# Seven-product stage with its own sum buffers, another product order, a bank-to-bank copy and weight buffers assigned by hand

## The chip, the cores and the metric

The kernel runs on one core of a Trainium2 chip. Its time is the device time of one execution in microseconds; the median of three runs is given. A profiled execution gives the trace, with times counted from its first instruction (the span). Engines are named as in the trace: PE is TensorE's matmuls and PEld its weight loads, DVE is VectorE, ACT ScalarE, POOL GpSimd, SP SyncE.

## The reference

Causal attention over 2 x 12 heads, 448 positions and a head dimension of 64, then two feed-forward layers over the 896 tokens:

```python
x = attention(q, k, v)                       # (896, 768)
r = np.maximum(x @ moe_w_in, 0.0)            # (896, 2048)
x = (s * (r * r) + b) @ moe_w_out            # (896, 768)
gate = 1.0 / (1.0 + np.exp(-(x @ w_gate)))   # (896, 1536)
out = (gate * (x @ w_val)) @ w_out           # (896, 768)
```

All inputs and the output are fp32. The weight matrices are handed over as the two 32-bit words of 64-bit numbers, which the kernel turns into floats itself.

## The kernel before

Tokens lie in the free dimension, in two halves of 448 (`B` = 2, `S` = 448); a matmul multiplies a 128x128 block of weights with a 128x448 block of activations. To keep fp32 accuracy every operand is split into a high and a low part, and a block product is three matmuls: high by high, high by low, low by high.

The stages follow each other on TensorE: attention, `w_in`, `w_out`, then the **seven-product stage** for `w_gate` and `w_val`, then two output stages for `w_out`. The seven-product stage computes, for each of 12 quads `q` (128 columns of the gate and of the value, both token halves), the four 128x448 results by Strassen and Winograd's scheme with seven products instead of eight. Each product has a depth of 3 blocks, so 3 x 3 = 9 matmuls, or 63 a quad. The left factors are combinations of weights: `a`, `b` (halves of the gate), `s1`, `s2` (the sum tile `s12`), `s3`, `s4` (`s34`) and `d` (half of the negated value); the right factors are combinations of activations (`b11`, `t1`, ..., `b22`), kept in `x2_b` and `z_b`. `PARTS` says which pair makes which product. Products 1, 6, 7, 4 are accumulated in bank A, 5 and 3 in bank C, 2 in bank E; after each of 1, 6 and 7 `evacuate` reads the running sum of bank A.

Per quad the weights come about so. SyncE loads `raw` (768 KB, two buffers). `float_steps` makes a float tile `wt` of it: one instruction on ScalarE (L77), four on VectorE (L79 to L91). VectorE adds the tiles to `s12` and `s34` (L593). `halves` splits a tile: ScalarE copies the high part (L102); the low part is either a subtraction on VectorE (L108) or, with `adder`, a negating copy on ScalarE (L105) and a GpSimd transfer that adds the tile to it (L106). `a`, `s12` and `d` take the adder, `s34` the subtraction. `wt`, `s12` and `s34` share a pool of five buffers, the split weights have another pool of five; a pool hands out its buffers in turn, and the first writer waits until the last reader of the old content is done.

The order of products is written out (`seq`), and `LEAD` says how many products ahead each step of a quad's weights stands in the program; within that, a scheduler at build time sets each engine's order. At run time each engine works through its list in order, so that one waiting instruction holds all behind it.

After the stage `split_y` splits the results `y_f` into blocks that are no longer needed (`free`), and two output stages multiply them (L711, L136).

## Time and profile before

| | us |
|---|---|
| median of 3 runs | 575.52 |
| lowest and highest | 573.78, 575.71 |
| profiled execution, own time | 580.73 |
| its span | 579.0 |
| mean granted TensorE clock in it | 0.991 |

The profiled execution lies 1.73 us above its span and 5.21 us above the median. TensorE is busy for 97% of the span, PEld 85%, VectorE 73%, ScalarE 56%. Busy times count an instruction from start to end; matmuls overlap, so that one takes 0.36 us from start to end but the next starts about 0.2 us after it.

### The profile page before, as it was taken

How to read it: one execution, taken by the hardware profiler on the slowest of the kernel's cores; microseconds unless marked ns; L12 is line 12 of the kernel's file. 1: busy time of each engine (PE TensorE's matmuls, PEld its weight loads, DVE VectorE, ACT ScalarE, POOL GpSimd, SP SyncE). 2: the span in 40 equal slices, each digit the busy share in tenths (PEclk: the TensorE clock that was granted, in tenths of full speed). 3: DMA queues.
4: the chain of work that ended last, by engine and by line, in shares of the span. 5: the costliest groups of instructions: out<-in, count | busy, mean ns of one | idle time of the engine just before them, and what ended most of it. 6: DMA issues, size and time to landing. Idle time of an engine off the chain costs nothing.

```text
span 579.0 us, 8350 instructions
## 1 busy us (share of the span) xinstructions
PE 560.4 (97%) x3068; PEld 490.4 (85%) x3069; DVE 421.6 (73%) x798; ACT 326.4 (56%) x622; POOL 73.3 (13%) x129
## 2 busy tenths in 40 slices
PE   8999999999999999999999999999989899999997
PEld 4666789899999999999999988888878789999996
DVE  5899676999999976865527788876777779987100
ACT  7989846776776633332227677665656588235100
POOL 3676600000000000000001111111201110000000
PEclk9999999999999999999999999998989899999999
DMA  7854012344444453233152577775766643456100
GB/s 242 304 167 174 19 60 106 115 158 164 155 144 148 147 170 121 72 137 109 53 112 48 143 182 182 183 178 153 180 171 169 166 94 121 154 167 200 41 33 32
DMA packets 21354, 79.19 MB, mean 137 GB/s; under 512 B 2624, under 2 KB 6080, under 8 KB 21312
## 3 DMA queue, kind: packets, MB, share of 16 engines
q1 hardware_dynamic: 15696, 65.94, 33.8%
q0 software_dynamic: 5184, 11.80, 11.5%
q10 hardware_dynamic: 432, 0.92, 0.5%
q8 instruction: 24, 0.39, 0.3%
q14 instruction: 18, 0.15, 0.1%
HBM read 64.10 MB, written 2.75 MB: 115 GB/s over the span
## 4 chain that ended last, share of the span: by engine, by line
PE 61%; issue 15%; DVE 9%; DMA 7%; ACT 6%; POOL 1%; POOLq 0%; DVEq 0%; ACTq 0%
PE acc L136 40%; PE acc L711 8%; DMA d_lo<-wt 5%; PE po L321 4%; PE tp L299 3%; PE sc L250 3%; DVE wt L91 2%; DVE wt L87 2%; ACT pt L240 2%; ACT wt L77 2%; PE bankA L627 2%; DMA a_lo<-wt 1%; POOL a_lo L106 1%; PE bankC L627 1%; DVE wt L79 1%
## 5 line engine op out<-in xcount | busy, mean ns | idle before, releaser
L136 PE MATMUL acc<-x_b,whi 128*128 128x448 f32 x456 | 130.8, 368 | 0.0
L77 ACT ACTIVATE wt<-raw 128x768 f32<-128x768 f32 (+1 forms) x70 | 62.2, 888 | 65.4 <-DMA raw<-in_w_out 14.3
L136 PE MATMUL acc<-gb,whi 128*128 128x448 f32 x336 | 96.6, 368 | 0.0
L136 PEld LDWEIGHTS acc<-x_b,whi 128*128 128x128 f32 x456 | 85.4, 188 | 8.1 <-ACT whi L102 0.3
L136 PE MATMUL acc<-x_b,wlo 128*128 128x448 f32 x228 | 83.8, 367 | 0.1
L79 DVE TENSOR_SCALAR wt<-wt 128x768 f32<-128x768 f32 (+1 forms) x70 | 38.8, 554 | 47.0 <-ACT wt L77 46.4
L136 PEld LDWEIGHTS acc<-gb,whi 128*128 128x128 f32 x336 | 63.1, 188 | 6.5
L102 ACT ACTIVATE whi<-wt 128x768 fp32r<-128x768 f32 (+1 forms) x46 | 37.5, 815 | 54.5 <-PE acc L136 39.7
L87 DVE SCALAR_TENSOR_TENSOR wt<-raw,wt 128x768 uint32<-128x768 uint32 (+1 forms) x70 | 65.7, 938 | 1.0
L91 DVE SCALAR_TENSOR_TENSOR wt<-raw,wt 128x768 uint32<-128x768 uint32 (+1 forms) x70 | 65.6, 937 | 0.7
L136 PE MATMUL acc<-gb,wlo 128*128 128x448 f32 x168 | 61.8, 368 | 0.0
L108 DVE TENSOR_TENSOR wlo<-wt,whi 128x768 fp32r<-128x768 f32 (+1 forms) x46 | 42.8, 930 | 16.9 <-ACT whi L102 16.8
L106 POOL DMA_DIRECT2D a_lo<-wt x12 | 10.4, 865 | 334.2 <-ACT a_lo L105 229.6
L136 PEld LDWEIGHTS acc<-x_b,wlo 128*128 128x128 f32 x228 | 42.8, 188 | 4.5 <-DVE wlo L108 0.5
L240 ACT ACTIVATE pt<-pt,m 128x320 f32<-128x320 f32 (+6 forms) x84 | 41.7, 500 | 5.5 <-DVE m L237 5.4
L279 POOL TENSOR_SCALAR pt<-pt,r 128x128 f32<-128x128 f32 (+6 forms) x82 | 39.9, 507 | 27.6 <-DVE r L274 21.7
L82 DVE TENSOR_SCALAR wt<-wt 128x768 uint32<-128x768 uint32 (+1 forms) x70 | 38.5, 550 | 1.4
L136 PEld LDWEIGHTS acc<-gb,wlo 128*128 128x128 f32 x168 | 31.5, 188 | 3.1
L237 DVE CUSTOM_DVE_ANT_0 pt<-sc,mask 128x320 f32<-128x320 f32 (+6 forms) x84 | 30.2, 412 | 4.4 <-PE sc L250 4.4
L627 PE MATMUL bankA<-x_b,s_hi 128*128 128x448 f32 x96 | 29.7, 373 | 0.0
L250 PE MATMUL sc<-qk 64*64 64x64 f32 (+6 forms) x336 | 26.0, 410 | 0.8 <-DMA qk<-in_qk 0.7
L102 ACT ACTIVATE s_hi<-s 128x768 fp32r<-128x768 f32 x24 | 20.3, 846 | 11.2 <-PE bankE L627 9.2
(125 smaller groups left out, 1059.8 us busy)
## 6 DMA issues: line engine op xcount, KB each, us to landing
raw<-in_w_in SPq DMA_DIRECT2D x16, 768.0 KB, 4.3
raw<-in_w_gate SPq DMA_DIRECT2D x12, 768.0 KB, 4.3
raw<-in_w_val SPq DMA_DIRECT2D x12, 768.0 KB, 4.9
raw<-in_w_out SPq DMA_DIRECT2D x12, 640.0 KB, 4.1
qk<-in_qk SPq DMA_DIRECT2D x9, 608.0 KB, 5.8
raw<-in_w_out SPq DMA_DIRECT2D x6, 768.0 KB, 4.4
a_lo<-wt POOLq DMA_DIRECT2D x12, 384.0 KB, 3.9
s_lo<-s POOLq DMA_DIRECT2D x12, 384.0 KB, 4.1
```

The source lines that it names most:

```text
L77: nc.scalar.activation(out=f32(tt), in_=f32(high), func=AF.Abs, scale=RAISE)
L79: nc.vector.tensor_scalar(out=f32(tt), in0=f32(tt), scalar1=F64_TINY, scalar2=F64_HUGE, op0=ALU.max, op1=ALU.min,)
L87: nc.vector.scalar_tensor_tensor(out=tt, in0=low, scalar=29, in1=tt, op0=ALU.logical_shift_right, op1=ALU.bitwise_or,)
L91: nc.vector.scalar_tensor_tensor(out=tt, in0=high, scalar=SIGN, in1=tt, op0=ALU.bitwise_and, op1=ALU.bitwise_xor,)
L102: nc.scalar.activation(out=hif, in_=f32(tt), func=AF.Copy)
L108: nc.vector.tensor_tensor(out=lof, in0=f32(tt), in1=f32(hif), op=ALU.subtract)
L136: nc.tensor.matmul(acc[:, :S], w[:, k - k0], m, start=k == 0 and i == 0, stop=k == K - 1 and i == 2)
L240: nc.scalar.activation(out=pc, in_=pc, func=AF.Exp, scale=-1.0, bias=m, accum_out=l)
L250: nc.tensor.matmul(sc[j * D:(j + 1) * D, :n], t["qk"][rows, q0:q0 + D], t["qk"][rows, k0:k0 + n], start=True, stop=True,)
L279: engine.tensor_scalar(out=probs(i, c), in0=probs(i, c), scalar1=st[i]["r"][:, c:c + 1], scalar2=1.0, op0=ALU.mult, op1=ALU.mult,)
L627: nc.tensor.matmul(acc[:, :S], a[:, j], m, start=fresh and j == 0 and n == 0, stop=j == KH - 1 and n == 2, skip_group_check=True,)
L711: nc.tensor.matmul(acc[d, h][:, :S], w[:, k * GROUP + d], m, start=u == 0 and k == 0 and n == 0, stop=u == NF2 // 2 - 1 and k == 1 and n == 2,
```

## The change

- The sums `s12` and `s34` get five places of their own (`s_f`) in a block of activations that is free by then, in place of the pool that they shared with `wt`. The activation blocks are cut in two for this (`ga0`, `ga1`, `gb00`, `gb01`, `gb10`, `gb11`).
- The order of products in a quad becomes 1, 5, 4 (of the quad before), 6, 3 (of the quad before), 2, 7; it was 6, 3 (before), 1 (next), 7, 2, 5 (next), 4. `LEAD` changes with it.
- After product 1 ScalarE copies bank A to bank E, and product 2 is added there by TensorE; the sigmoid then reads bank E. Before, product 1 was copied to SBUF and VectorE added bank E.
- Split weights: `a`/`b` alternate between two buffers, `s12` has one, `s34` alternates between two, `d` has one of its own in `ga1`. `s12` and `d` now use the subtraction, `s34` the adder. `raw` and `wt` keep two and five buffers.
- The blocks for the split outputs are taken from other places.

```diff
--- before.py
+++ after.py
@@ -32,6 +32,7 @@
     B, NP, _, W = qk.shape
     S = outT.shape[1] // B
     AHEAD = 2
+    SLOTS = 5
     READY = 3
     U = 6
     NT = B * S
@@ -44,7 +45,7 @@
 
     const = ctx.enter_context(tc.tile_pool(name="const", bufs=1))
     big = ctx.enter_context(tc.tile_pool(name="big", bufs=1))
-    wp = ctx.enter_context(tc.tile_pool(name="wp", bufs=AHEAD + READY))
+    wp = ctx.enter_context(tc.tile_pool(name="wp", bufs=1))
     ev = ctx.enter_context(tc.tile_pool(name="ev", bufs=4))
     BANKS = {"w": 7, "po": 1}
     dram = ctx.enter_context(tc.tile_pool(name="dram", bufs=1, space=bass.MemoryType.DRAM))
@@ -61,8 +62,14 @@
     def bank(name, tag):
         return ps.tile([P, 512], F32, tag=tag, name=name, bufs=BANKS[tag])
 
+    turns = {}
+
+    def turn(what, n):
+        turns[what] = turns.get(what, -1) + 1
+        return f"{what}{turns[what] % n}"
+
     def load_words(src, n):
-        raw = wp.tile([P, U * P, 2], U32, tag="raw", name="raw", bufs=2)
+        raw = wp.tile([P, U * P, 2], U32, tag=turn("raw", 2), name="raw")
         nc.sync.dma_start(out=raw[:, :n * P], in_=src)
         return raw
 
@@ -71,7 +78,7 @@
 
         nn = n * P
         low, high = raw[:, :nn, 0], raw[:, :nn, 1]
-        t = wp.tile([P, U * P], U32, tag="wt", name="wt")
+        t = wp.tile([P, U * P], U32, tag=turn("wt", SLOTS), name="wt")
         tt = t[:, :nn]
         out.append(t)
         nc.scalar.activation(out=f32(tt), in_=f32(high), func=AF.Abs, scale=RAISE)
@@ -92,10 +99,12 @@
             out=tt, in0=high, scalar=SIGN, in1=tt, op0=ALU.bitwise_and, op1=ALU.bitwise_xor,
         )
 
-    def halves(tt, out, adder=False, name="w"):
-
-        hi = wp.tile([P, U, P], F32R, tag="whi", name=f"{name}hi")
-        lo = wp.tile([P, U, P], F32R, tag="wlo", name=f"{name}lo")
+    def halves(tt, out, adder=False, name="w", slot=None):
+
+        if slot is None:
+            slot = turn("w", SLOTS)
+        hi = wp.tile([P, U, P], F32R, tag=f"{slot}h", name=f"{name}hi")
+        lo = wp.tile([P, U, P], F32R, tag=f"{slot}l", name=f"{name}lo")
         out += [hi, lo]
         nn = tt.shape[1]
         hif, lof = (x.rearrange("p k m -> p (k m)")[:, :nn] for x in (hi, lo))
@@ -151,8 +160,9 @@
 
     x_b = blocks(big, KC * B, "x", "x_b")
     ga = ctx.enter_context(tc.tile_pool(name="ga", bufs=1))
-    ga_b = blocks(ga, AHEAD * B, "ga", "ga_b")
+    ga_b = [blocks(ga, AHEAD * B - 1, "ga0", "ga0"), blocks(ga, 1, "ga1", "ga1")]
     gb_b = []
+    FIRST = (9, NF2)
 
     def pair_of(t, i):
         return t[:, i, 0], t[:, i, 1]
@@ -161,7 +171,12 @@
         return pair_of(x_b, B * k + h)
 
     def at_g(k, h):
-        return pair_of(ga_b, B * k + h) if k < AHEAD else pair_of(gb_b[h], k - AHEAD)
+        if k < AHEAD:
+            n = B * k + h
+            return pair_of(ga_b[0], n) if n < AHEAD * B - 1 else pair_of(ga_b[1], 0)
+        one, two = gb_b[h]
+        k -= AHEAD
+        return pair_of(one, k) if k < FIRST[h] else pair_of(two, k - FIRST[h])
 
 
     def first_evac(f, h, acc):
@@ -476,7 +491,10 @@
                 pass
 
     gb = ctx.enter_context(tc.tile_pool(name="gb", bufs=1))
-    gb_b += [blocks(gb, NF1 - AHEAD, f"gb{h}", f"gb{h}") for h in range(B)]
+    gb_b += [
+        [blocks(gb, n, f"gb{h}{i}", f"gb{h}{i}") for i, n in enumerate((FIRST[h], NF1 - AHEAD - FIRST[h]))]
+        for h in range(B)
+    ]
 
     for f in range(AHEAD, NF1):
         ready = [(*split[f], 0, KC)] if f < AHEAD + READY else units(w_in[f], KC)
@@ -551,7 +569,9 @@
     done[end] = [bank("acc", "w") for _ in range(B)]
     for unit in last_units:
         mm3(done[end][0], unit, NF1, at_g, 0)
-    z_b = blocks(gb, NF1 - AHEAD, "gb0", "z_b")
+    z_b = blocks(gb, FIRST[0], "gb00", "z_b")
+    SUMS = 5
+    s_f = gb.tile([P, SUMS, U * P], F32, tag="gb01", name="s_f")
     for i, key in enumerate(late):
         place[key] = (z_b, i)
     for ty, j in late:
@@ -569,34 +589,37 @@
 
         t = quads[q] = {}
         fl = []
-        yield from drained(float_steps(load_words(w_gate[q], KC), KC, fl))
-        yield from drained(float_steps(load_words(w_val[q], KC), KC, fl, negate=True))
-        tg, tv = fl
         H = KH * P
         one, two = slice(0, H), slice(H, 2 * H)
 
-        def split(tt, names, adder):
+        def split(tt, names, adder, slot):
             out = []
-            for _ in halves(tt, out, adder, names[0] + "_"):
+            for _ in halves(tt, out, adder, names[0] + "_", f"w{slot}"):
                 pass
             for n, ty in enumerate(names):
                 t[ty] = [x[:, n * KH:(n + 1) * KH] for x in out]
 
-        split(tg, ("a", "b"), True)
+        yield from drained(float_steps(load_words(w_gate[q], KC), KC, fl))
+        split(fl[0], ("a", "b"), True, q % 2)
         yield
-        s12 = wp.tile([P, U * P], U32, tag="wt", name="s12")
-        s34 = wp.tile([P, U * P], U32, tag="wt", name="s34")
+        yield from drained(float_steps(load_words(w_val[q], KC), KC, fl, negate=True))
+        tg, tv = fl
+        s12, s34 = (s_f[:, (2 * q + n) % SUMS] for n in range(2))
         for out, x, y in (
-            (s12[:, one], tv[:, one], tv[:, two]), (s12[:, two], s12[:, one], tg[:, one]),
-            (s34[:, one], tg[:, one], tv[:, one]), (s34[:, two], s12[:, two], tg[:, two]),
+            (s12[:, one], f32(tv[:, one]), f32(tv[:, two])), (s12[:, two], s12[:, one], f32(tg[:, one])),
+            (s34[:, one], f32(tg[:, one]), f32(tv[:, one])), (s34[:, two], s12[:, two], f32(tg[:, two])),
         ):
-            nc.vector.tensor_tensor(out=f32(out), in0=f32(x), in1=f32(y), op=ALU.add)
+            nc.vector.tensor_tensor(out=out, in0=x, in1=y, op=ALU.add)
         yield
-        split(s12, ("s1", "s2"), True)
+        split(s12, ("s1", "s2"), False, 2)
         yield
-        split(s34, ("s3", "s4"), False)
+        split(s34, ("s3", "s4"), True, 4 - q % 2)
         yield
-        split(tv[:, two], ("d",), True)
+        d_w = ga.tile([P, 2, KH, P], F32R, tag="ga1", name="d_w")
+        hi, lo = (d_w[:, n].rearrange("p k m -> p (k m)") for n in range(2))
+        nc.scalar.activation(out=hi, in_=f32(tv[:, two]), func=AF.Copy)
+        nc.vector.tensor_tensor(out=lo, in0=f32(tv[:, two]), in1=f32(hi), op=ALU.subtract)
+        t["d"] = d_w[:, 0], d_w[:, 1]
         yield
 
     def drained(steps):
@@ -617,7 +640,7 @@
         wh, wl = quads[q][w]
         xs = x2_at(x)
         key = {1: "A", 6: "A", 7: "A", 4: "A", 5: "C", 3: "C", 2: "E"}[i], q
-        fresh = i in (1, 5, 2)
+        fresh = i in (1, 5)
         if fresh:
             banks[key] = bank(f"bank{key[0]}", "w")
         acc = banks[key]
@@ -632,28 +655,33 @@
     def evacuate(i, q):
 
         A, C, E = (banks[x, q][:, :S] if (x, q) in banks else None for x in "ACE")
-        if i in (1, 6, 7):
+        if i == 1:
+            E = banks["E", q] = bank("bankE", "w")
+            nc.scalar.activation(out=E[:, :S], in_=A, func=AF.Copy)
+        elif i == 2:
+            s = ring[i, q] = r_f[:, ring["n"] % RING]
+            ring["n"] += 1
+            nc.scalar.activation(out=s, in_=E, func=AF.Sigmoid)
+        elif i in (6, 7):
             s = ring[i, q] = r_f[:, ring["n"] % RING]
             ring["n"] += 1
             nc.scalar.activation(out=s, in_=A, func=AF.Copy)
         if i == 7:
             s = ring[7, q]
             nc.vector.tensor_tensor(out=s, in0=C, in1=s, op=ALU.add)
-        elif i in (2, 3):
-            s = ring[1 if i == 2 else 6, q]
-            nc.vector.tensor_tensor(out=s, in0=E if i == 2 else C, in1=s, op=ALU.add)
+        elif i == 3:
+            s = ring[6, q]
+            nc.vector.tensor_tensor(out=s, in0=C, in1=s, op=ALU.add)
             nc.scalar.activation(out=s, in_=s, func=AF.Sigmoid)
-            if i == 3:
-                nc.vector.tensor_tensor(out=y_f[:, B * q + 1], in0=s, in1=ring[7, q], op=ALU.mult)
+            nc.vector.tensor_tensor(out=y_f[:, B * q + 1], in0=s, in1=ring[7, q], op=ALU.mult)
         elif i == 4:
-            nc.vector.tensor_tensor(out=y_f[:, B * q], in0=A, in1=ring[1, q], op=ALU.mult)
-
-    seq = [(1, 0), (2, 0), (5, 0)]
-    for q in range(NF2 + 1):
-        for i, n in ((6, q), (3, q - 1), (1, q + 1), (7, q), (2, q), (5, q + 1), (4, q)):
-            if 0 <= n < NF2 and (i, n) not in seq:
-                seq.append((i, n))
-    LEAD = (9, 8, 6, 5, 3, 0, -2)
+            nc.vector.tensor_tensor(out=y_f[:, B * q], in0=A, in1=ring[2, q], op=ALU.mult)
+
+    seq = [(1, 0), (5, 0), (6, 0), (2, 0), (7, 0)]
+    for q in range(1, NF2 + 1):
+        seq += [(1, q), (5, q), (4, q - 1), (6, q), (3, q - 1), (2, q), (7, q)]
+    seq = [(i, q) for i, q in seq if q < NF2]
+    LEAD = (10, 8, 8, 6, 3, 2, -3)
     todo = sorted(
         (seq.index((1, q)) - lead, q, n) for q in range(NF2) for n, lead in enumerate(LEAD)
     )
@@ -667,18 +695,21 @@
     for unit in last_units:
         mm3(done[end][1], unit, NF1, at_g, 1)
     second_half(d, done[end], ("t2", "t4"))
-    RING = 2 * B * AHEAD
+    RING = 2 * (B * AHEAD - 1)
     ring["n"] = 0
-    r_f = ga.tile([P, RING, S], F32, tag="ga", name="r_f")
-    y_f = gb.tile([P, B * NF2, S], F32, tag="gb1", name="y_f")
+    r_f = ga.tile([P, RING, S], F32, tag="ga0", name="r_f")
+    y_f = gb.tile([P, B * NF2, S], F32, tag="gb10", name="y_f")
+    v_b = blocks(gb, NF1 - AHEAD - FIRST[1], "gb11", "v_b")
     for n, (i, q) in enumerate(seq):
         prepare(n)
         multiply(i, q)
         evacuate(i, q)
 
 
-    free = [(z_b, i) for i in range(len(late), NF1 - AHEAD)]
+    free = [(v_b, i) for i in range(NF1 - AHEAD - FIRST[1])]
     free += [place[ty, j] for ty in ("b11", "t1", "t2", "t3", "b21", "t4", "b22") for j in range(KH)]
+    c_b = blocks(ga, AHEAD * B - 1, "ga0", "c_b")
+    free += [(c_b, i) for i in range(AHEAD * B - 1)]
 
     def at_y(k, h):
         return pair_of(*free[B * k + h])
```


Lines shift: L77 is now L84, L79 to L91 are L86 to L98, L102 to L108 are L111 to L117, L593 is L612, L627 is L650, L711 is L742.

TensorE, where product 1 of a quad begins, before. `bankA_3400` belongs to the new quad, `bankA_3283` to the one before it; `a` is product 1's weight, `s3` product 7's:

```order
L627 MATMUL bankC_3216<-z_b_2963,s3_lo_3175 128x448
L627 MATMUL bankA_3400<-x2_b_2162,a_hi_3294 128x448 x2
L627 MATMUL bankA_3283<-x2_b_2162,s3_hi_3279 128x448 x2
L627 MATMUL bankA_3283<-x2_b_2162,s3_lo_3280 128x448
L627 MATMUL bankA_3283<-x2_b_2162,s3_hi_3279 128x448
L627 MATMUL bankA_3400<-x2_b_2162,a_lo_3295 128x448
L627 MATMUL bankA_3400<-x2_b_2162,a_hi_3294 128x448 x2
L627 MATMUL bankA_3400<-x2_b_2162,a_lo_3295 128x448
L627 MATMUL bankA_3400<-z_b_2963,a_hi_3294 128x448 x2
```

Here the first two matmuls of product 1 need only `a_hi`; three of product 7 follow, then the first that needs `a_lo`. After the change the same place reads so, with `bankA_3416` for the new quad and `bankA_3304` for the one before it, and `d_w` for product 4's weight:

```order
L650 MATMUL bankA_3416<-z_b_2966,a_hi_3280 128x448 x2
L650 MATMUL bankA_3416<-z_b_2966,a_lo_3281 128x448
L650 MATMUL bankA_3304<-x2_b_2165,d_w_3340 128x448
L650 MATMUL bankC_3432<-x2_b_2165,s1_hi_3353 128x448 x2
L650 MATMUL bankC_3432<-x2_b_2165,s1_lo_3354 128x448
L650 MATMUL bankC_3432<-x2_b_2165,s1_hi_3353 128x448 x2
L650 MATMUL bankC_3432<-x2_b_2165,s1_lo_3354 128x448
L650 MATMUL bankC_3432<-z_b_2966,s1_hi_3353 128x448 x2
L650 MATMUL bankC_3432<-z_b_2966,s1_lo_3354 128x448
L650 MATMUL bankA_3304<-x2_b_2165,d_w_3340 128x448 x2
L650 MATMUL bankA_3304<-z_b_2966,d_w_3340 128x448 x6
```

Product 7 no longer stands beside product 1. One matmul of product 4 of the old quad comes right after product 1 of the new one, then product 5 (`bankC`), then the other eight of product 4.

ScalarE, one quad before (`wt<-raw` makes floats, `a`, `d`, `s1`, `s3` are split weights, `r_f<-bankA` reads bank A, `r_f<-r_f` is a sigmoid, `z_b` an output split):

```order
L102 ACTIVATE s3_hi_3396<-s34_3316 128x768
L689 ACTIVATE z_b_2963<-y_f_3084 128x448
L102 ACTIVATE a_hi_3411<-wt_3360 128x768
L105 ACTIVATE a_lo_3412<-a_hi_3411 128x768
L102 ACTIVATE d_hi_3427<-wt_3261 128x384
L638 ACTIVATE r_f_3083<-bankA_3400 128x448
L105 ACTIVATE d_lo_3428<-d_hi_3427 128x384
L645 ACTIVATE r_f_3083<-r_f_3083 128x448
L102 ACTIVATE s1_hi_3460<-s12_3432 128x768
L105 ACTIVATE s1_lo_3461<-s1_hi_3460 128x768
L77 ACTIVATE wt_3477<-raw_3475 128x768
L77 ACTIVATE wt_3495<-raw_3493 128x768
```

ScalarE, one quad after the change, from the copy of `d`'s high part to the copy of bank A after product 7:

```order
L620 ACTIVATE d_w_3564<-wt_3399 128x384
L84 ACTIVATE wt_3695<-raw_3693 128x768
L668 ACTIVATE r_f_3077<-bankA_3528 128x448
L111 ACTIVATE s1_hi_3577<-s_f_2967 128x768
L84 ACTIVATE wt_3735<-raw_3733 128x768
L111 ACTIVATE s3_hi_3601<-s_f_2967 128x768
L114 ACTIVATE s3_lo_3602<-s3_hi_3601 128x768
L111 ACTIVATE a_hi_3616<-wt_3583 128x768
L675 ACTIVATE r_f_3077<-r_f_3077 128x448
L664 ACTIVATE r_f_3077<-bankE_3538 128x448
L114 ACTIVATE a_lo_3617<-a_hi_3616 128x768
L668 ACTIVATE r_f_3077<-bankA_3528 128x448
```

`wt_3399`, from which `d` is made, is the value tile of this quad, `wt_3695` and `wt_3735` are the tiles of the quad three later, and `a_hi_3616` is for two quads later. The `wt_3695` tile takes the buffer of `wt_3399`. The copy after product 7 stands last; the negating copy for `d` is gone.

## Rows read from the trace of the kernel before

**Rows 1.** The head of the page: the span, and TensorE and the other engines in it.

```profile
span 579.0 us, 8350 instructions
PE 560.4 (97%) x3068; PEld 490.4 (85%) x3069; DVE 421.6 (73%) x798; ACT 326.4 (56%) x622; POOL 73.3 (13%) x129
```

**Rows 2.** Stretches cut at TensorE's waits: length, busy of PE, PEld, DVE, ACT, POOL, clock, DMA share, GB/s.

```profile
362.81:376.91 14.10, 13.03 (x64) 11.76 (x64) 11.66 (x19) 9.66 (x15) 2.54 (x4) 1.00 0.70 183
376.91:391.92 15.01, 13.03 (x64) 11.76 (x64) 11.12 (x18) 9.20 (x14) 3.10 (x4) 1.00 0.76 178
391.92:407.65 15.73, 14.78 (x63) 13.05 (x64) 11.08 (x18) 9.33 (x14) 1.93 (x3) 0.89 0.59 157
```

**Rows 3.** What TensorE waited for: total us, times, longest.

```profile
PE bankA L627 <- DMA a_lo<-wt: 12.9, 10, 2.0
```

**Rows 4.** Timeline of one quad: start, length, instruction, idle time and releaser; PE, ACT, POOL.

```profile
420.32 0.37 PE L627 MATMUL bankA<-x_b,s_hi 128*128 128x448 f32 x1
422.50 0.47 PE L627 MATMUL bankA<-x_b,a_lo 128*128 128x448 f32 x1 [1.81 <-DMA a_lo<-wt]
...
415.65 0.85 ACT L102 ACTIVATE a_hi<-wt 128x768 fp32r<-128x768 f32 x1 [2.80 <-PE bankA L627]
416.53 0.85 ACT L105 ACTIVATE a_lo<-a_hi 128x768 fp32r<-128x768 f32 x1
...
417.91 0.53 ACT L638 ACTIVATE r_f<-bankA 128x448 f32<-128x448 f32 x1
418.33 0.52 ACT L105 ACTIVATE d_lo<-d_hi 128x384 fp32r<-128x384 f32 x1
...
417.78 0.87 POOL L106 DMA_DIRECT2D a_lo<-wt  x1 [9.50 <-PE bankA L627]
```

**Rows 5.** The chain that ended last: start, length, what, number of instructions.

```profile
105.79 183.57 PE acc L136 x887
...
473.33 1.82 PE bankC L627 x9
...
487.92 43.78 PE acc L711 x216
```

**Rows 6.** Groups by line and form, 340 to 460 us: count, busy us, mean ns, idle.

```profile
L77 ACT ACTIVATE wt<-raw 128x768 f32<-128x768 f32 x16 | 14.5, 907 | 10.2 <-DMA a_lo<-wt 8.4 <-DMA d_lo<-wt 1.7
...
L102 ACT ACTIVATE s_hi<-s 128x768 fp32r<-128x768 f32 x16 | 13.6, 848 | 8.3 <-PE bankE L627 8.3
...
L638 ACT ACTIVATE r_f<-bankA 128x448 f32<-128x448 f32 x24 | 12.2, 532 | 2.9 <-PE bankA L627 2.9
...
L645 ACT ACTIVATE r_f<-r_f 128x448 f32<-128x448 f32 x16 | 9.1, 567 | 0.0
...
L593 DVE TENSOR_TENSOR s<-wt 128x384 f32<-128x384 f32 x16 | 8.1, 550 | 0.0
L108 DVE TENSOR_TENSOR s_lo<-s,s_hi 128x768 fp32r<-128x768 f32 x8 | 7.6, 951 | 0.0
```

**Rows 7.** Timeline: a last matmul of product 4, and VectorE reading its bank.

```profile
328.31 0.36 PE L627 MATMUL bankA<-z_b,d_lo 128*128 128x448 f32 x1
...
328.71 0.62 DVE L649 TENSOR_TENSOR y_f<-bankA,r_f 128x448 f32<-128x448 f32 x1 [0.71 <-PE bankA L627]
```

**Rows 8.** The raw tile, 330 to 470 us: landing, and the transfers of value weights.

```profile
DMA to landing us min/median/max: 4.2/4.4/5.9
...
raw<-in_w_val SPq DMA_DIRECT2D x8, 768.0 KB, 4.9
```

**Rows 9.** Timeline at the start of the seven-product stage: PE, then ACT.

```profile
313.59 0.57 PE L627 MATMUL bankA<-x_b,a_hi 128*128 128x448 f32 x2
...
317.31 0.57 PE L627 MATMUL bankC<-x_b,s_hi 128*128 128x448 f32 x2
...
317.06 0.53 ACT L638 ACTIVATE r_f<-bankA 128x448 f32<-128x448 f32 x1
...
320.58 1.28 ACT L645 ACT_TABLE_LOAD   x1
```

## The prediction

> **What bounds the kernel now.** I read the page's head first: TensorE is busy for 560.4 of 579.0 us [rows 1], so only a stage in which TensorE waits can give anything back. The list of what TensorE waited for has one large entry, the bank A matmuls of the seven-product stage waiting for the adder transfer that finishes `a_lo`: ten waits, 12.9 us [rows 3]. They repeat once a quad. The table of stretches cut at these waits shows what a quad costs [rows 2]: 14.10 us where the wait is short, 15.01 where it is long, and 15.73 in the quad after a long one, where the granted clock averages 0.89, so that 0.11 × 15.73 = 1.7 us is lost to a stretch at the 1.2 GHz level. Three of the nine quads that lie between such waits are of that last kind, 5.2 us together; each follows a wait of 1.8 to 2.0 us, and none follows a wait of about 1.0.
>
> Why TensorE waits is read from the timeline of one quad [rows 4]. ScalarE idles 2.80 us until product 4 of the quad before has freed its weight buffer (the pool of five hands the next `a` tile the buffer that `d` held). Then `a_hi` takes 0.85 us, `a_lo` 0.85, GpSimd issues at 417.78, and TensorE resumes at 422.50, 6.85 us after ScalarE began. In that time it has two products and six matmuls to do, 24 × 0.2027 = 4.87 us. The difference is 2.0 us; the row shows 1.81 because it counts from the end of the matmul before, and the next could have begun 0.2 us earlier. The other engines have room: VectorE is busy 11.1 to 11.7 us and ScalarE 9.2 to 9.7 us per quad [rows 2], against 63 matmuls × 0.2027 = 12.77 us.
>
> The pitch 0.2027 us comes from the chain that ended last: 216 matmuls in 43.78 us [rows 5], and nine in 1.82. An earlier stretch of the same chain has 887 in 183.57, 0.2070 each, both at full granted clock. TensorE thus has two rhythms 2% apart; the kernel was in the slow one up to 322 us and in the fast one after its first pauses.
>
> The stage runs from 313.59 [rows 9] to 487.92 [rows 5]: 174.3 us. 12 quads × 7 products × 9 matmuls = 756, × 0.2027 = 153.2 us. The rest, 21.1 us, is 12.9 of waits, 5.2 of half clock, and 3.0 that I put mainly on what the list of waits leaves out at each of them (a quad of 14.10 us with a wait of about 1.1: 14.10 − 12.77 − 1.1 = 0.2).
>
> **The change, part by part.** *The weight buffers.* `a` and `b` now alternate between two buffers. The one for quad q+2 is free when product 2 of quad q ends, and product 1 of quad q+2 starts eight products later: 8 × 9 × 0.2027 = 14.6 us for the 6.85 us chain above. The ten waits go. The other buffers by the same count: `s12` has four products (7.3 us) for a copy and a subtraction (0.85 + 0.95 us) [rows 6], `s34` eight products for the adder path, `d` (one buffer) six products (10.9 us) for two short operations. None of these can hold TensorE. With the waits go the half-clock stretches, since all three followed a long wait.
>
> *Engine work.* VectorE gains the subtraction for `d` (0.55 us, the price of a 128x384 operation [rows 6]) and loses the addition of bank E (0.62 us, the price of a 128x448 operation [rows 7]); `s12` and `s34` swap paths at equal price. ScalarE loses one negating copy (0.52 us [rows 4]). GpSimd issues two adder transfers a quad in place of three. So both engines stay at or a little under their present 11.7 and 9.7 us, under 12.77.
>
> *The copy from bank A to bank E.* No row shows ScalarE writing a bank. It is nearest to the copy from a bank to SBUF, 0.53 us [rows 6]; as the lower bound I take nothing, as the upper 0.85, the 768-column copy. Where product 6 follows two products after product 1 (3.65 us), all of these are hidden. The Trainium skill, page "ScalarE: Activation LUTs", section "Step-by-step: what each stage is for", says that ScalarE reaches PSUM faster than SBUF as a destination. No run here shows it yet; by it the copy is under 0.53 us, and the sum moves by less than the first wait below.
>
> *The new tight place: bank A is read out three times a quad and multiplied into again.* TensorE's new order puts product 7 of quad q−1, product 1 of q, and then one matmul of product 4 of q−1. That matmul waits for ScalarE's copy of bank A after product 7, and everything behind it on TensorE waits too. Count from S, the start of the last matmul of the previous product 4. Its result reaches VectorE 0.40 later [rows 7]; `y_f` and the `d` subtraction follow (0.62 + 0.55, with the usual small overlap), so ScalarE begins `wt` for quad q+3 at S + 1.5, because the buffer of that `wt` held the values that `d` was made from. Before the copy in question ScalarE has in its queue: two `wt` of 0.91, a bank copy of 0.53, `s1_hi`, `s3_hi`, `s3_lo`, `a_hi`, `a_lo` at 0.85, and two sigmoids of 0.57 [rows 4, 6]; with the copy itself 8.27 us. Independent ScalarE instructions start 0.11 us before the last one ends (417.91 to 418.33 for 0.53 [rows 4]), a dependent one 0.03 after; ten handovers, nine of them independent, make it 7.3. The copy ends at S + 8.8. TensorE gets there at S + 0.20 + 45 × 0.2027 = 9.3. Spare: 0.5 us. Without any overlap the queue ends at 9.8 and TensorE waits 0.45 us in each of ten quads, 4.5 us. I take the overlapped value, since the timeline shows it [rows 4], and 0.6 us in all for a few late quads.
>
> The Trainium skill, page "Perfetto Trace Analysis", section "Matmuls" under "Optimizing Tensor Performance", asks that matmul groups rotate through banks so that reading out one overlaps the next group. This speaks against the new order. By the rows the nine matmuls between (1.82 us) and the queue's place cover the copy; by the rule it would be exposed, which is the second rival.
>
> *The start of the stage.* Product 6 of quad 0 now comes third and needs the copy A to E. TensorE gets there where it began its third product before, at 317.31; on ScalarE the copy stands where the old copy of bank A stood, 317.06 to 317.59 [rows 9]: a wait of 0.3 us. The table load of 1.28 us [rows 9] now stands between product 2's and product 7's copies and makes the first matmul of product 4 wait; between 0 and 1.3, I take 0.3.
>
> *The end of the stage.* There is no product 1 and 5 of a thirteenth quad, so product 4 of the last follows its product 7 after only five matmuls of the output product. ScalarE has two output splits and the copy to do first: 0.46 + 0.46 + 0.53, from about 0.4 after the last matmul's start, against 0.2 + 5 × 0.2027. A wait of 0.6 us; 0 if the splits come earlier, 1.0 if the copy is later.
>
> *Output splits* of all but two blocks must now wait for the last quad's products. The first output product needs only the first four blocks, free 14 us before; the later ones have 7.3 us each. Hidden; without that cover each split would cost 0.6 us on VectorE.
>
> *Sum:* 153.2 + 0.3 + 0.3 + 0.6 + three times that 0.2 + 0.6 for late quads = 155.6 us in place of 174.3, a gain of 18.7. The profiled execution took 580.73 us, so 562.0. The runs timed without a profile have a median of 575.52, 5.2 us under the profiled one, just the price of the three half-clock stretches; I read that as runs that mostly lacked them, so the forecast stands against the median as 13.5 us faster.
>
> **Rivals.**
> 1. *The slow rhythm.* With no pauses to jolt it, TensorE stays at 0.2070 through the stage and the 432 matmuls after it: 1,188 × 0.0043 = 5.1 us more, 567. For it: 105 to 322 us ran so without a pause [rows 5]. Against it: small pauses at the start remain.
> 2. *ScalarE's queue exposes the copy of bank A*, 0.45 to 0.9 us a quad: 566 to 571. For it: only 0.5 us spare. Against it: the row-by-row count.
> 3. *The load of the next value weights becomes the loop* (slower than before). With two `raw` buffers this load is issued only when VectorE has finished the last step of the previous quad's values, which now stands behind its addition for product 7, which waits for the copy of bank A, which stands behind that very `wt` on ScalarE. From `wt` (S + 3.5) to the copy's end (8.8), plus 0.62 + 0.95 on VectorE, plus the landing: 6.9 + 4.9 = 11.8 us, under 12.77. Landings reach 5.9 [rows 8], which costs nothing or 0.1 us. To be slower than before it must lose 13.5 us, 1.3 a quad, so landings of 7.2 us would have to be the rule: 576. Nothing here shows one.
> 4. *Even the early stages take the fast rhythm*, 887 × 0.0043 = 3.8 us less: 558. Nothing in the change touches them.
> 5. *The stall only moves*: some other buffer waits just as long, no change. The counts above leave at least 5 us for each.
>
> **How the numbers follow.** Chances: forecast 0.52 (559.5 to 564.5), rival 1 0.20, rival 2 0.18, rival 3 0.03, rival 4 0.05, rival 5 0.02. The likeliest gives 562.0. A range from 558.5 to 569 holds the forecast, rival 1 and two thirds of rival 2. Within 0.5% (2.9 us, about what a measurement of this kernel can tell from no change) of 575.5 falls rival 5 and little else. Faster 0.95, same 0.02, slower 0.03.
>
> **What would show it.** In the new profile TensorE's waits for the adder transfer should be gone, quads should follow each other at 12.8 to 13.0 us, and the granted clock should be full throughout. Three small waits should stand near 317, 325 and the end of the stage. The first matmul of product 4 shows rivals 1 and 2 apart: idle time before it, released by ScalarE, is rival 2; none, with matmuls 0.207 apart, is rival 1. The prediction is wrong if `wt` on ScalarE waits for a `raw` load in most quads, or if TensorE waits on VectorE's `y_f`.

## The result, and the profile after

The changed kernel takes 566.60 us (median of 4 runs, 565.18 to 568.90) against 575.62 for the kernel before (4 runs beside it, 573.78 to 576.81): a ratio of 0.985, with a 95% interval of 0.9801 to 0.9899. That is 9.0 us faster where 13.5 was forecast, inside the range of 558.5 to 569 and 4.6 us above the forecast of 562.0. The profiled execution took 565.19 us, its span is 563.2.

The head of its page answers to [rows 1]:

```profile
span 563.2 us, 8265 instructions
PE 551.8 (98%) x3069; PEld 486.6 (86%) x3069; DVE 423.1 (75%) x798; ACT 315.1 (56%) x610; POOL 63.4 (11%) x117
```

and the list of what TensorE waited for (us in total, times, longest) to [rows 3]:

```profile
PE bankA L650 <- ACT r_f L668: 5.0, 6, 1.5
...
PE bankA L650 <- ACT bankE L660: 0.2, 1, 0.2
```

The ten waits for the adder transfer are gone, and with them the half clock (mean granted clock 0.999, before 0.991). In their place stand six waits of the first matmul of product 4 for ScalarE's copy of bank A. Stretches cut at that matmul (to within 0.2 us of it where it did not wait), with the columns of [rows 2], show what a quad costs now (the first, four from the middle, the last of eleven):

```profile
320.93:333.61 12.68, 12.68 (x63) 11.77 (x64) 12.36 (x21) 9.55 (x16) 1.75 (x2) 1.00 0.54 160
...
347.94:362.73 14.79, 13.29 (x63) 11.75 (x64) 12.16 (x20) 9.04 (x15) 1.78 (x3) 1.00 0.76 210
...
376.45:389.37 12.92, 12.91 (x63) 11.76 (x64) 11.69 (x19) 8.30 (x13) 1.96 (x3) 1.00 0.64 152
389.37:403.46 14.09, 13.38 (x66) 11.83 (x64) 11.21 (x19) 8.46 (x14) 1.47 (x3) 1.00 0.71 206
403.46:416.49 13.03, 13.03 (x64) 11.76 (x64) 11.40 (x19) 8.25 (x13) 1.70 (x3) 1.00 0.63 149
...
456.67:469.23 12.56, 12.45 (x59) 11.00 (x59) 12.56 (x22) 11.33 (x22) 0.00 (x0) 1.00 0.40 110
```

The eleven quads take (469.23 − 320.93) / 11 = 13.48 us on average, where 12.77 was forecast; no engine is busy for more than 13.4 of any of them. What sets most of them is in the chain that ended last, here one turn of it between two loads of value weights (start, length, what):

```profile
405.40 5.63 DMA raw<-in_w_val
...
411.11 0.09 ACT wt L84
411.20 0.72 issue
411.92 0.84 ACT s_hi L111
...
412.79 0.85 ACT s_lo L114
413.64 0.74 ACT a_hi L111
414.37 0.47 ACT r_f L675
...
414.87 0.04 DVE y_f L676
414.91 0.51 issue
415.41 0.56 DVE wt L89
...
416.00 0.96 DVE wt L94
...
417.41 0.96 DVE wt L98
...
418.43 6.30 DMA raw<-in_w_val
```

Read it downwards: the load lands, ScalarE takes its first step on the values, then two splits and `a_hi`, then the sigmoid of product 3. VectorE's multiplication by that sigmoid (L676) stands between its own steps on the values, so these wait too, and only after the last of them (L98) is the raw buffer free for the next load. From landing (411.03) to the next issue (418.43) this is 7.4 us, and with the landing of 5.63 the turn is 13.03. Of the seven value loads issued in the stage after 330 us, ScalarE's first step on the values waited for six, 7.3 us in all, as the list of what ScalarE waited for between 325 and 460 us has it:

```profile
ACT wt L84 <- DMA raw<-in_w_val: 7.3, 6, 1.7
```

ScalarE is then late with everything behind it, the copy of bank A last. Not every quad over 12.77 is a wait: in the stretch from 376.45 TensorE is busy throughout and still takes 12.9 us, because its matmuls start 0.2067 us apart there (below).

The three pieces of the same chain that answer to [rows 5] and [rows 9] settle where the rest of the time went:

```profile
105.43 203.76 PE acc L145 x1004
...
471.32 1.83 PE bankC L650 x9
473.15 42.76 PE acc L742 x211
```

The stage runs from 309.22 to 473.15, less five matmuls of the output product that now lie inside it (216 − 211): 162.9 us, before 174.3, forecast 155.6. It began 4.4 us earlier than before, although nothing ahead of it was meant to change: 203.76 / 1004 = 0.2029 us a matmul in the stages before it, where [rows 5] have 0.2070. That is 4.0 us; the other 0.4 lie ahead of those matmuls (105.43 for 105.79). What follows the stage is as long as before. So of the 15.8 us between the spans 11.4 are from the stage and 4.4 from what lies ahead of it.

### The profile page after: what moved, and what is told of

Read it like the earlier page. It is cut to its first block, busy times and chain, and to the rows that moved or that the text cites. A ratio compares the mean times of both kernels' runs of the same rounds, so it can differ in the third digit from the quotient of the medians.

```text
span 563.2 us, 8265 instructions
## 1 busy us (share of the span) xinstructions
PE 551.8 (98%) x3069; PEld 486.6 (86%) x3069; DVE 423.1 (75%) x798; ACT 315.1 (56%) x610; POOL 63.4 (11%) x117
## 4 chain that ended last, share of the span: by engine, by line
PE 68%; ACT 11%; DVE 10%; DMA 8%; issue 3%; ACTq 0%; SPq 0%; DVEq 0%
PE acc L145 44%; PE acc L742 8%; DMA raw<-in_w_val 6%; PE po L336 4%; PE tp L314 3%; PE bankA L650 3%; PE sc L265 3%; DMA raw<-in_w_out2a 2%; DVE wt L98 2%; DVE wt L94 2%; ACT pt L255 2%; PE bankC L650 2%; ACT s_lo L114 1%; ACT s_hi L111 1%; DVE wt L89 1%
## 5 line engine op out<-in xcount | busy, mean ns | idle before, releaser
L84 ACT ACTIVATE wt<-raw 128x768 f32<-128x768 f32 (+1 forms) x70 | 61.8, 883 | 77.1 <-DMA raw<-in_w_out2b 16.9
L94 DVE SCALAR_TENSOR_TENSOR wt<-raw,wt 128x768 uint32<-128x768 uint32 (+1 forms) x70 | 65.8, 939 | 1.5
L98 DVE SCALAR_TENSOR_TENSOR wt<-raw,wt 128x768 uint32<-128x768 uint32 (+1 forms) x70 | 65.6, 937 | 0.8
L86 DVE TENSOR_SCALAR wt<-wt 128x768 f32<-128x768 f32 (+1 forms) x70 | 38.8, 555 | 31.1 <-ACT wt L84 30.8
L111 ACT ACTIVATE whi<-wt 128x768 fp32r<-128x768 f32 (+1 forms) x46 | 37.3, 811 | 40.6 <-PE acc L145 28.4
L117 DVE TENSOR_TENSOR wlo<-wt,whi 128x768 fp32r<-128x768 f32 (+1 forms) x46 | 42.6, 928 | 18.2 <-ACT whi L111 17.9
L650 PE MATMUL bankA<-x_b,s_hi 128*128 128x448 f32 x96 | 27.5, 368 | 0.2 <-ACT bankE L660 0.2
L726 ACT ACTIVATE ot<-acc 128x448 f32<-128x448 f32 x12 | 6.5, 543 | 36.5 <-PE acc L145 33.2
L265 PE MATMUL sc<-qk 64*64 64x256 f32 (+6 forms) x336 | 25.3, 401 | 1.2 <-DMA qk<-in_qk 1.1
```

Of the source, the lines that this page charges most:

```text
L84: nc.scalar.activation(out=f32(tt), in_=f32(high), func=AF.Abs, scale=RAISE)
L94: nc.vector.scalar_tensor_tensor(out=tt, in0=low, scalar=29, in1=tt, op0=ALU.logical_shift_right, op1=ALU.bitwise_or,)
L98: nc.vector.scalar_tensor_tensor(out=tt, in0=high, scalar=SIGN, in1=tt, op0=ALU.bitwise_and, op1=ALU.bitwise_xor,)
L111: nc.scalar.activation(out=hif, in_=f32(tt), func=AF.Copy)
L117: nc.vector.tensor_tensor(out=lof, in0=f32(tt), in1=f32(hif), op=ALU.subtract)
L265: nc.tensor.matmul(sc[j * D:(j + 1) * D, :n], t["qk"][rows, q0:q0 + D], t["qk"][rows, k0:k0 + n], start=True, stop=True,)
```

## The experiments

**Theory A:** the load of the value weights is a loop, landing plus some 7.4 us on ScalarE and VectorE, and longer than TensorE's 12.77. **Theory B:** ScalarE's queue ahead of the copy of bank A is too long by itself (rival 2 of the prediction). Each kernel below is the changed kernel with the edit shown; where an order is held, `after(x, y)` adds an edge that makes x follow y on their engine and waits for nothing. Kernels measured together share the runs of the kernel before, whose median was 573.03, 575.45, 573.48 and 572.74 us in the four groups that follow.

**The changed kernel again.**

> The changed kernel a second time, for its spread and a second trace. Both theories: 565 to 569 us, with some six waits at the first matmul of product 4 behind ScalarE's copy of bank A, 4 to 6 us in all. If the rhythm of the early stages differs from execution to execution, the pitch from 105 to 309 us is 0.2027 in a trace whose span is near 563 and 0.2070 in one near 567.

566.55 us (6 runs, 565.32 to 569.55; ratio 0.9876, interval 0.9831 to 0.9921). Seven waits at the same place, 6.8 us in all. Its early stages show 0.2029 again, but the span is 565.0 because of the longer waits, so the span alone doesn't tell the rhythm.

**The old order with the new buffers** (the product order, lead times and evacuation of the kernel before):

```diff
-    seq = [(1, 0), (5, 0), (6, 0), (2, 0), (7, 0)]
...
-    LEAD = (10, 8, 8, 6, 3, 2, -3)
...
+    seq = [(1, 0), (2, 0), (5, 0)]
...
+    LEAD = (9, 8, 6, 5, 3, 0, -2)
```

> The buffers of the change alone: its slots for split weights, its own buffers for the sums and for d, and d split without the adder, but the order of products, the lead times and the evacuation of products 1 and 2 of the kernel before. Theory A (the two alternating buffers for a and b are what ended the ten waits): no wait of bank A for the adder transfer, no half clock, 560 to 568; what is left is a loop or small waits of this order's own. Theory B (the buffers only work with the new order of products): waits of 1 us and more a quad for another split weight remain, 570 to 578.

583.31 us, 1.0125 of the kernel before (1.0066 to 1.0184). The waits for `a_lo` are back in what TensorE waited for:

```profile
PE bankA L650 <- DMA a_lo<-wt: 14.5, 9, 2.4
```

Two transfers issued 0.2 us apart in a waiting quad (KB each, us to landing), from the list of transfers of this run, show why the waits are no shorter:

```profile
raw<-in_w_val SPq DMA_DIRECT2D x1, 768.0 KB, 8.1
a_lo<-wt POOLq DMA_DIRECT2D x1, 384.0 KB, 8.1
```

In the old order ten products run from product 1 to product 2 of a quad, both counted, so a buffer of an alternating pair is free for only four, 7.3 us; the new order holds it for six and leaves eight. In that quad `a_hi` began at 400.31, when the buffer was free, and TensorE's wait ended at 410.54, 10.2 us later. The buffers alone are worth nothing here. Theory B of this run holds, though the time lies 5 us above its range.

**A third raw buffer.** From quad 3 on, every third load goes into a tile of the released activations:

```diff
-        raw = wp.tile([P, U * P, 2], U32, tag=turn("raw", 2), name="raw")
...
+        raw = (gb if third else wp).tile([P, U * P, 2], U32, tag="gb11" if third else turn("raw", 2), name="raw")
```

> A third buffer for raw weights in the seven-product stage, so that the load of a quad's values no longer waits for the last step on the values of the quad before. Theory A (the load of the value weights is a loop: landing 5.6 to 6.9 us, then 7.3 us on ScalarE and VectorE until the next issue, 13.0 to 14.3 us for a quad that TensorE could do in 12.8): the loads are issued several us earlier, the waits of product 4 for the bank A copy fall from 5.0 us to under 1.0, the quads come at 12.8 to 13.0 us, the time is 6 to 7 us under the changed kernel, 558 to 562. Theory B (ScalarE's queue by its own length exposes the copy): the waits stay at 0.4 to 0.9 us a quad, no difference beyond 1 us, 565 to 569.

590.79 us (ratio 1.0282, 1.0228 to 1.0336). This says nothing on either theory: with the load early, the scheduler put the first step on the values ahead of other work on ScalarE, where it waits for its weight buffer. What TensorE waited for in this run:

```profile
PE bankA L650 <- ACT r_f L668: 22.2, 15, 2.9
```

and one such step in its timeline of ScalarE (start, length, and in brackets how long it waited for what):

```profile
409.31 0.91 ACT L84 ACTIVATE wt<-raw 128x768 f32<-128x768 f32 x1 [7.25 <-DMA a_lo<-wt]
```

**The same, with the order held.**

```diff
+    for q in range(NF2 - 3):
+        after(("abs", q + 3), ("s1", q + 1))
```

> The third raw buffer again, but with the first step on a quad's values held on ScalarE behind the first half of the s12 split of two quads before, where the changed kernel has it; the order of the engines' instructions in the steady quads is then that of the changed kernel, and only the load comes earlier. Theory A (the load of the values is a loop of landing plus 7.3 us): that first step no longer waits for its load, the waits of product 4 for the bank A copy fall from 5.0 and 6.8 us to under 1.5, the time is 4 to 6 us under the changed kernel, 560 to 563. Theory B (ScalarE's queue is too long by itself): the load waits on ScalarE, 0.3 to 1.7 us a quad, become idle time elsewhere, the waits of product 4 stay at 4 us or more, 565 to 569.

563.29 us (ratio 0.9813, 0.9776 to 0.9851), 3.3 under the changed kernel; product 4 waits four times, 3.6 us. No step on the values waits for its load any more; four wait for the adder transfer of `a_lo`, which still reads the buffer (3.9 us). The time moved as A says, though its interval overlaps that of the changed kernel's second measurement (0.9831 to 0.9921). The waits lie between the two theories: behind the raw buffer stood the next buffer.

**The multiplication on GpSimd.**

```diff
-            nc.vector.tensor_tensor(out=y_f[:, B * q + 1], in0=s, in1=ring[7, q], op=ALU.mult)
+            nc.gpsimd.tensor_tensor(out=y_f[:, B * q + 1], in0=s, in1=ring[7, q], op=ALU.mult)
```

> The multiplication that closes product 3 (y_f) done by GpSimd in place of VectorE, so that VectorE's steps on the values don't stand behind the sigmoid; every other order of instructions in the steady quads stays. Theory A: from a load's landing to the next issue it takes 0.9 + 0.6 + 0.6 + 0.9 + 1.0 and some 0.5 for an addition between, 4.5 us in place of 7.3; with a landing of 5.6 to 6.9 us that is 10.1 to 11.4, under 12.8: the waits of product 4 for the bank A copy fall from 5.0 us to under 1.0 and the time is 5 to 7 us under the changed kernel, 558 to 562. Theory B: ScalarE's queue is as long as it was, so no difference beyond 1 us, 565 to 569.

567.14 us (ratio 0.9894): no gain, waits 7.3 us. The timeline of two turns on VectorE shows two reasons, and GpSimd's row belongs to the first:

```profile
378.05 1.67 DVE L89 TENSOR_SCALAR wt<-wt 128x768 uint32<-128x768 uint32 x1
...
394.10 0.62 DVE L671 TENSOR_TENSOR r_f<-bankC,r_f 128x448 f32<-128x448 f32 x1 [1.42 <-ACT r_f L668]
394.64 0.95 DVE L98 SCALAR_TENSOR_TENSOR wt<-raw,wt 128x768 uint32<-128x768 uint32 x1
...
377.93 1.37 POOL L676 TENSOR_TENSOR y_f<-r_f 128x448 f32<-128x448 f32 x1
```

A step of 0.56 us takes 1.67 while GpSimd multiplies. And with L676 out of the way, the addition for product 7 (L671) is the next in the row between the steps; it waits for the copy of bank A. That is the path that rival 3 of the prediction named. So the run moved the loop to another path and does not test it further.

**Values first on VectorE.** Both of these behind the last step on the values, with the order on ScalarE held as above:

```diff
+        after((3, q - 1), ("v", q + 3))
+        after((7, q), ("v", q + 3))
```

> Two raw buffers as in the changed kernel; on VectorE the multiplication after product 3's sigmoid and the addition for product 7 stand behind the last step on the values instead of between its steps, all other orders in the steady quads unchanged. Theory A: the next load is issued about 1.5 us earlier (the four steps follow each other, 0.6 + 0.6 + 0.9 + 1.0 us, without a wait for ScalarE), the loop takes 11.5 to 12.3 us and no longer holds TensorE: waits of product 4 under 1.5 us in all, 560 to 563. Theory B: no difference beyond 1 us, 565 to 569.

573.82 us (12 runs, ratio 0.9988, 0.9959 to 1.0017), waits of 11.6 us: worse than the changed kernel, and outside both ranges. The loads are issued earlier, and so at the same time as the others. Four transfers issued within 4.2 us (387.91 to 392.02) in its list of transfers:

```profile
raw<-in_w_gate SPq DMA_DIRECT2D x1, 768.0 KB, 4.5
raw<-in_w_val SPq DMA_DIRECT2D x1, 768.0 KB, 8.3
s_lo<-s_f POOLq DMA_DIRECT2D x1, 384.0 KB, 6.1
a_lo<-wt POOLq DMA_DIRECT2D x1, 384.0 KB, 9.1
```

The order did what it was meant to: from ScalarE's first step on the values to the next load of values it is 4.3 us at 386.7 and 4.6 at 401.1, where the changed kernel has 7.3. But these steps wait mostly for another transfer, in the list of what ScalarE waited for between 325 and 460 us:

```profile
ACT wt L84 <- DMA a_lo<-wt: 17.6, 6, 6.8
...
ACT wt L84 <- DMA raw<-in_w_val: 4.1, 2, 2.1
```

The step writes a weight buffer that the adder transfer of `a_lo` for an earlier quad still reads. So there is a second loop beside theory A's: `a_lo` lands, the step on the values begins, and the next `a_lo` stands behind it on ScalarE (issued at 392.02, landed at 401.09, the next issued at 406.4). In the changed kernel it was never the last to end, but close: before the six waits there `a_lo` landed 0.2 to 3.4 us ahead of the load.

**The copy of bank A first**, ahead of bank E's sigmoid and `a_lo` on ScalarE:

```diff
+        after(("sigmoid", q), ("copy", 7, q))
+        after(("a_lo", q + 2), ("copy", 7, q))
+        after((7, q), ("v", q + 3))
```

(here `("v", q + 3)` is the step L94, so that the addition keeps its place).

> The copy of bank A after product 7 stands on ScalarE ahead of bank E's sigmoid and of a_lo, 1.2 us earlier in the queue; the loop of the value load is untouched (the addition for product 7 keeps its place on VectorE). Theory B: the queue ahead of the copy is shorter by more than its excess of 0.4 to 0.9 us, so the waits of product 4 all but vanish and the time is 4 to 6 us under the changed kernel, 560 to 563. Theory A: TensorE runs at the loop's period whatever the copy's place, so the gain is at most the 1.2 us once, and waits of 4 us or so remain: 564 to 568.

568.84 us (ratio 0.9899), waits of 8.0 us: 1.2 us less ahead of the copy gives nothing back. ScalarE's first step on the values still waits five times for its load, 7.9 us in all. Theory B falls.

**No bank copy.**

```diff
-        fresh = i in (1, 5)
+        fresh = i in (1, 5, 2)
...
+            nc.vector.tensor_tensor(out=s, in0=E if i == 2 else C, in1=s, op=ALU.add)
```

> The changed kernel without the copy from bank to bank: product 2 starts its own bank E, product 1 is copied to SBUF and VectorE adds the two, as in the kernel before; everything else of the change stays. If the copy is only another place for the same ScalarE work, VectorE has 0.62 us more a quad and all of it hidden: 565 to 569. Theory A (the loop through VectorE's steps sets the quad): the addition stands between steps of the gate and value weights and lengthens the loop by 0.3 to 0.6 us a quad, 568 to 573.

566.07 us (ratio 0.987, 0.9827 to 0.9913), as the changed kernel. Copying bank to bank is worth nothing that can be measured here. Theory A's range for this run, 568 to 573, was missed: the loop that I expected to lengthen did not cost more.

**The third raw buffer, and `a_lo` by subtraction.**

```diff
-        split(fl[0], ("a", "b"), True, q % 2)
+        split(fl[0], ("a", "b"), False, q % 2)
```

> As the kernel with the third raw buffer and the held order, and a_lo made by a subtraction on VectorE in place of ScalarE's negating copy and the adder transfer. It takes away what the trace of that kernel shows next (ScalarE's first step on the values waiting for the adder transfer of a_lo, which reads the weight buffer that the step writes: four times about 1 us) and one of the four transfers that a quad has under way at once. Theory C (after the raw buffer, the four transfers that run together are the limit: each lands in 5 to 9 us where alone it took about 4): landings of the values under 4.9 us and of s_lo under 4.5, waits of product 4 under 1.5 us in all, 557 to 561. Rival D (VectorE, with 0.95 us more a quad, is full): no gain, 562 to 567.

562.39 us (561.85 to 563.17; ratio 0.9802, 0.9765 to 0.9838). TensorE waits once in the stage, 1.5 us in quad 0, and then never. Two of its quads, as above:

```profile
352.35:365.11 12.76, 12.76 (x64) 11.83 (x63) 12.09 (x20) 7.58 (x12) 1.06 (x1) 1.00 0.61 161
365.11:377.88 12.77, 12.77 (x65) 11.84 (x63) 12.11 (x20) 7.58 (x12) 1.07 (x1) 1.00 0.57 149
```

The time lies in rival D's range, 562 to 567, and the rows tell the two apart: VectorE at 12.1 of 12.77 is not full and TensorE does not wait after quad 0, so rival D falls. The landings did not shorten as I expected (values 5.3, `s_lo` 7.3): they no longer matter, because no step on the weights waits for them. The time missed its 557 to 561 by the rhythm: this trace has the slow one, 4.0 us more, up to the start of the stage.

**The subtraction alone**, without the third buffer:

> The changed kernel with a_lo made by a subtraction on VectorE, no third raw buffer. It parts the two edits of the kernel that lost its waits. Theory A (the loop of the value load, through one raw buffer): the loop keeps its landing of 5.3 to 6.2 us, and the subtraction (0.95 us) now stands between the steps on the values, 7.3 + 0.9 = 8.2 us; 13.5 us and more a quad, waits of product 4 of 6 to 15 us in all, 567 to 574. Rival (it was the adder transfer alone that held the weight buffers): waits under 2 us, 560 to 563.

560.82 us (560.23 to 561.56; ratio 0.9782, 0.9744 to 0.9821), with waits of 2.5 us. My size was wrong, and the rival's range, 560 to 563, holds the time. The loop of the value load is there all the same, now through L671 again, but three quads at 12.77 pass before it holds TensorE, and one turn is 13.55: landing 5.32, then 8.2. The chain of that turn:

```profile
389.56 5.32 DMA raw<-in_w_val
...
399.07 0.43 ACT r_f L668
...
399.97 0.62 DVE r_f L671
...
403.11 5.01 DMA raw<-in_w_val
```

So each of the two edits gives a part: the subtraction brings fewer transfers and a shorter ScalarE queue, which starts the loop later; only the buffer ends it.

**A sixth weight buffer** in place of the subtraction (one slot of the buffer for sums):

```diff
-    SUMS = 5
+    SUMS = 4
...
+        yield from drained(float_steps(load_words(w_val[q], KC, q >= 3 and (2 * q + 1) % 3 == 0), KC, fl, True, s_f[:, SUMS].bitcast(U32) if q >= 3 and q % 3 == 2 else None))
```

> As the kernel with the third raw buffer and the held order, with a sixth weight buffer for float weights (in the place of one of the five buffers for sums), so that neither gate nor value weights wait for a buffer that the adder transfer of a_lo or d still reads; the transfers stay as many. Theory C, buffers alone: the four waits of about 1 us on the adder transfer go, but the transfers still run together; waits of product 4 under 1.5 us in all, 558 to 562. Rival: the gate's first steps, free to start earlier, stand ahead of bank copies on ScalarE and make product 4 or 7 wait: 564 or more.

583.28 us (ratio 1.0152, 1.0104 to 1.02). The orders on ScalarE moved again, as the rival of this run expected (564 or more). The execution that was profiled lay 8 us above the median, so its times are not read here, and the cause stays open.

**The best of them**, with the gate's first step of quad 3 held behind the first copy after product 6:

```diff
+    after(("gate", 3), ("copy", 6, 0))
```

> The kernel with the third raw buffer and the subtraction, and on ScalarE the gate's first step of quad 3 held behind the copy of bank A after product 6 of quad 0, which waited 1.5 us for it. Both theories: that wait goes, nothing else moves much: 561 to 562 in the median, a span near 559 where the early stages keep the slower pitch and near 555 where they keep the faster.

556.95 us (556.12 to 562.71; ratio 0.9729, 0.9684 to 0.9773), 9.6 under the changed kernel's second median and the fastest of all. The 1.5 us went, and more: 561 to 562 was expected. Five of the six executions have spans of 554.3 to 555.5, which the expectation gave for the fast rhythm; none of them was traced. The one execution that was traced is the one of 562.71, and its quads are as even as those above, but longer:

```profile
337.42:350.44 13.02, 13.02 (x64) 11.82 (x63) 12.58 (x20) 7.60 (x12) 0.88 (x1) 1.00 0.51 145
350.44:363.46 13.02, 13.02 (x64) 11.82 (x63) 12.16 (x20) 7.60 (x12) 0.84 (x1) 1.00 0.53 145
```

## Why the prediction was right, and where it was off

**The waits that go** were right: none of the ten is left, and the clock is full. With the same buffers in the old order, where the count of products between two uses is four and not eight, the waits are back; that run also put back the lead times and the evacuation, of which the evacuation alone changes nothing (566.07). I had put this under the buffers; it belongs to buffers and order together.

**Engine work and the bank copy** were right in the main: the copy from bank to bank took 0.536 us where I had taken 0.53, and ScalarE stays under the forecast's 9.7 us a quad until the output splits begin. VectorE reached 12.4 where 11.7 was forecast, but that is still under 12.77. The Trainium skill, page "ScalarE: Activation LUTs", section "Step-by-step: what each stage is for", would have a copy into a bank faster than the copy to SBUF. That one took 0.533 in the same trace, so the measurement doesn't bear it out for a tile read from a bank.

**The small waits** came in their places: 0.24 at the start, where 0.3 was forecast, and about 0.3 each, by the starts of the matmuls, behind the table load and at the end of the stage (0.3 and 0.6 forecast).

**The step that failed** is in rival 3: "6.9 + 4.9 = 11.8 us, under 12.77. Landings reach 5.9 [rows 8], which costs nothing or 0.1 us." The first term was nearly right by size, 7.4 for 6.9, though its path runs through the sigmoid of product 3 and not through the copy of bank A. The second was carried over from a trace in which the transfers were spaced otherwise. In the changed kernel the landings of the values from quad to quad are 5.2 to 6.9 us. One quad's four transfers, issued at 387.03 (gate), 391.07 (values), 386.69 (`s_lo`) and 389.05 (`a_lo`):

```profile
raw<-in_w_gate SPq DMA_DIRECT2D x1, 768.0 KB, 5.3
raw<-in_w_val SPq DMA_DIRECT2D x1, 768.0 KB, 6.9
s_lo<-s_f POOLq DMA_DIRECT2D x1, 384.0 KB, 7.5
a_lo<-wt POOLq DMA_DIRECT2D x1, 384.0 KB, 8.7
```

Before, gate and value loads were 2.3 us apart and the first adder transfer 2.9 us behind, and it landed in 3.9. The new order has the four within 4.4 us here, and within 4.4 to 5.4 in the other quads. One quad later, with issues at 400.1, 405.4, 401.0 and 403.4, the same four landed in 4.1, 5.6, 5.0 and 4.6. That transfers close together slow each other is read from such rows, here, in the old order and with the values first; no run changed the spacing alone. The Trainium skill, page "DMA: Bandwidth & Descriptors", section "SWDGE vs HWDGE vs iDMA", says that SyncE's loads and GpSimd's transfers feed different queues of the same DMA engines, which serve them in turn. The rows fit that.

With 12.6 to 14.3 us for a turn, the loop held TensorE, and the stage took 7.3 us more than forecast (162.9 for 155.6). Not all of this is the loop. By the starts of its matmuls TensorE paused for about 8.4 us in the stage, of which the forecast had 2.4, and matmuls that started 0.2067 apart add 1.2: some 6 us are the loop's, and 1.2 are rival 1's slow rhythm in a part of the stage.

**The place** was rival 2's (idle time before the first matmul of product 4, released by ScalarE), the mechanism rival 3's; the sign of being wrong that the prediction gave, `wt` on ScalarE waiting for a raw load in most quads, came true for six of the seven value loads. That the copy is late by its own queue was tested and fell.

**The rhythm** went the other way ahead of the stage: rival 4, which had 0.05, gave 4.0 us back. The same order of matmuls has been traced in either rhythm (below), so one profiled execution decides no such rival.

**Luck.** That the number lies in the range is in part luck. The range reached to 569 for rivals 1 and 2, and not for the loop, which had 0.03 and was put at nothing. Without the 4.0 us of rival 4 the profiled execution would have taken about 569 by estimate (565.2 + 4.0), at the range's end.

**The sum**: 562.03 + 7.3 − 4.4 = 564.9, the profiled execution took 565.19. With the loops removed and the slow rhythm in the early stages, as the forecast had it, the kernel with the third buffer and the subtraction takes 562.39, near the forecast, though the subtraction relieves ScalarE besides: the sum was that of a kernel without either loop.

## What to carry to other kernels

A buffer's count is not enough: count the products between its last use and its next, in the new order, for the raw loads too, and for every reader of the buffer, the adder transfer too. A landing time cannot be carried along with its transfer to another place; where a change brings transfers together, take their landings from the worst row in which they overlapped, and add the steps that another engine's order puts between landing and release. And where one wait is removed, hold the order of the engines before judging: the scheduler may spend the freedom on something worse.

## What was not expected of the hardware

**TensorE's two rhythms change at its pauses.** Of fourteen traces, seven have the early stages at 0.2029 to 0.2030 us a matmul and seven at 0.2069 to 0.2070, all at full granted clock. The order of the matmuls does not decide it: the changed kernel and the one with the multiplication on GpSimd have the same order there, one at 0.2029 and one at 0.2069. Within a trace the rhythm changes where TensorE paused, and it changes either way. In the changed kernel's stage the matmuls start 0.2067 apart from 347.9 to 362.7, 376.5 to 403.5, 416.5 to 430.2 and 456.7 to 469.2, and 0.2027 apart elsewhere; each of these times is a pause at the first matmul of product 4, though not every pause changes it. The kernel with the third buffer and the subtraction is slow up to its first pause in the stage, and takes 12.77 us a quad from 339.6 on; the best kernel keeps 13.02 through the stage in the traced execution, past its one pause of 0.2 us. That the rhythm differs between executions of one kernel is likely but not shown: no kernel was traced in both, the best kernel's other five executions are 5 to 7 us shorter than its traced one, and the six with the third buffer and the subtraction lie within 1.3 us. What sets it stays open.

**GpSimd held VectorE up**: a step of 0.56 us took 1.67 beside a GpSimd multiplication of 1.37, and steps slowed like it (1.5 to 2.1 us) stand in four of nine turns. The Trainium skill, page "SBUF — State Buffer", section "Who interferes with whom", describes a port pair that the two share and that one of them holds for a whole instruction. The rows agree: VectorE's step began 0.12 us after the multiplication and ended 0.42 us after its end.

**A wait's length alone does not drop the clock.** In the changed kernel's second trace a wait of 2.22 us was followed by a quad at full clock, where before, waits of 1.8 to 2.0 were followed by half clock. That wait in the timeline of TensorE:

```profile
363.64 0.47 PE L650 MATMUL bankA<-x_b,d_w 128*128 128x448 f32 x1 [2.22 <-ACT r_f L668]
```

and the quad behind it in the table of stretches of the same trace:

```profile
363.60:376.60 13.00, 12.96 (x63) 11.76 (x63) 11.42 (x19) 8.30 (x13) 1.73 (x3) 1.00 0.58 129
```
